# Other start addresses for the activation tiles of a chained attention, MoE and gated MoE kernel

## The chip, the core and the metric

The kernel runs on one core of one Trainium2 chip. The metric is the time of one execution on the device in microseconds, lower is better; two executions of the kernel before took 691.92 and 691.20 us, so its median is 691.56 us. Besides these there is one profiled execution, whose rows are read below.

## What is computed

Three layers follow each other. The attention has 2 batches, 8 heads, 768 positions and a head size of 64, with a window of 96 positions and 8 global ones; its output is a matrix of 1536 tokens by 512. Two feed-forward layers work on that matrix. Everything is in 32-bit floats.

```python
def _moe_ref(x, w_in, w_out):              # 512 -> 2048 -> 512
    h = x @ w_in
    g = h * (1.0 / (1.0 + np.exp(-h)))
    return (g @ w_out).astype(np.float32)

def _moe2_ref(x, w_gate, w_val, w_out):    # 512 -> 1536 -> 512
    gate = 1.0 / (1.0 + np.exp(-(x @ w_gate)))
    val = x @ w_val
    return (gate * val @ w_out).astype(np.float32)

x = attention(q, k, v).reshape(1536, 512)
out = _moe2_ref(_moe_ref(x, ...), ...)
```

## The kernel before

**Split numbers.** In the two feed-forward layers each 32-bit operand is kept as two `float32r` parts, a high part and a low part. A product is three matmuls: weight high by data high, weight high by data low, weight low by data high. `mm3` (line 501) issues such a triple. So the tiles of these layers have a middle axis of 2: `X[g]` is 128 x 2 x 4 x 512 (three of them, one for each group of 512 tokens), a weight tile `W[n]` is 128 x 2 x 512, a tile `g` of gated activations is 128 x 2 x 512.

**Stages.** In the first 70 us or so attention runs with a few matmuls of the first layer between. `warm_up` (line 893) puts matmuls of a zeroed bf16 tile, whose results nobody reads, between the pieces of attention in the first part. In the window that follows, attention and the first layer are interleaved by `PLAN`. After that `phase_rest` (line 630) runs the remaining tasks: A1 and A2 (first layer), B1 and B2 (second layer), each for groups of 512 tokens and chunks of 128 hidden columns. A task is an `H` and a `Y`. `H` multiplies `X[g]`, as the operand that is streamed (moving), by a weight tile that is held (stationary): 12 matmuls of 512 columns into one PSUM bank in A, 24 into two banks in B. `act1` or `act2` makes the tile `g` from it on ScalarE and VectorE. `Y` multiplies `g` by the output weights: 12 matmuls, three for each of four PSUM banks. In A the weight tile is held and `g` is streamed (line 680); in B `g` is held and the weight tile is streamed (line 682). The `Y` of a task is issued one or two tasks after its `H`. Every one of these matmuls has its own weight load.

**Which group runs when.** A1 runs with group 2 alone, from about 202 us; then the groups come in order: A2 with groups 0, 1, 2 (their `H` from 245, 289 and 333 us), B1 with 0, 1, 2 (from 377, 430 and 480 us), B2 with 0, 1, 2 (from 530, 580 and 630 us).

**Where the tiles lie.** Pools hand out SBUF in the order of allocation. Per partition, `X[g]` takes 16384 bytes, `acc` 8192, `nm_all` 12 x 8 x 4 = 384, a weight tile 4096, a stage tile 4096, a `u` or `sg` tile 2048, a `g` tile 4096. All but `nm_all` are multiples of 256 bytes, and `nm_all` lies between `X` and `W`. So every `X` tile lies 128 bytes from every weight tile, counted modulo 256, and every `g` tile lies at 0 from it. Slices inside a tile begin at multiples of 512 bytes, so this holds for every operand of every matmul. The weight tiles 16 to 23, allocated later, keep the same place modulo 256.

**What orders the work.** The code gives each engine's instructions in the order of the calls, and a scheduler that simulates engine times settles the order within the attention part.

The lines that the change touches are the allocation of `X` (line 75), `act1` (line 518) and `act2` (line 532), which allocate `g`:

```python
X = [main.tile([128, 2, KD, G], F32R, name=f"x{g}") for g in range(NG)]
gt = g_p.tile([128, 2, 512], F32R, tag="g", name="g")
```

Of the kernel before, what the change touches and what calls it, by code (L numbers as in the profile page):

```python
# [8 lines left out]
F32 = mybir.dt.float32  # L9
F32R = mybir.dt.float32r  # L10
# [22 lines left out]
def attn_moe_moe2_kernel(  # L33
# [14 lines left out]
    nc = tc.nc  # L48
# [5 lines left out]
    G = 512  # L54
    NG = NT // G
    BPG = G // 128
    KD = DM // 128
# [6 lines left out]
    main = fast.enter_context(tc.tile_pool(name="main", bufs=1))  # L64
    stage_p = fast.enter_context(tc.tile_pool(name="stage", bufs=3))
    u_p = fast.enter_context(tc.tile_pool(name="up", bufs=2))
    g_p = fast.enter_context(tc.tile_pool(name="gp", bufs=4))
# [4 lines left out]
    ident = const.tile([128, 128], F32, name="ident")  # L72
    nval = const.tile([128, 4], F32, name="nval")
    flag = const.tile([1, 1], I32, name="flag")
    X = [main.tile([128, 2, KD, G], F32R, name=f"x{g}") for g in range(NG)]
    acc = [main.tile([128, 4, 512], F32, name=f"acc{g}") for g in range(2)]
    nm_all = main.tile([128, NBLK, H], F32, name="nm_all")
    W = [main.tile([128, 2, 512], F32R, name=f"w{n}") for n in range(16)]
# [16 lines left out]
    def defer(n, fn):  # L95
        seq[0] += 1
        deferred.append((clock[0] + n, seq[0], fn))
# [359 lines left out]
    def take(n):  # L457
# [7 lines left out]
        pv = ps.rearrange("p (a b) -> p a b", a=NP)  # L465
        nc.scalar.activation(out=X[g][:, 0, :, xs], in_=pv, func=AF.Copy)
        nc.vector.tensor_tensor(X[g][:, 1, :, xs], pv, X[g][:, 0, :, xs].bitcast(F32), ALU.subtract)
        if 0 < i < BLK - 1:
# [28 lines left out]


    g_t = {}

    def mm3(ps, wl, wsl, xl, xsl, first, last, order=((0, 0), (0, 1), (1, 0))):
        for j, (a, b) in enumerate(order):
            nc.tensor.matmul(  # L503
                ps, wl[(slice(None), a) + wsl], xl[(slice(None), b) + xsl],
                start=(first and j == 0), stop=(last and j == len(order) - 1),
            )

    def h_units(g, key, ps, cols=slice(0, G), free=True):
        need_w(key)
        w = wtile(key)  # L510
        for kk in range(KD):
            def f(kk=kk):
                mm3(ps, w, (slice(kk * 128, (kk + 1) * 128),), X[g], (kk, cols), kk == 0, kk == KD - 1)
                if kk == KD - 1 and free and g == NG - 1:
                    done_w(key)
            yield f

    def act1(tag, ps, lo_pool):
        gt = g_p.tile([128, 2, 512], F32R, tag="g", name="g")
        g_t[tag] = gt  # L520
        sg = e_p.tile([128, 512], F32, tag="sg", name="sg")
        if lo_pool:
            nc.scalar.activation(out=sg, in_=ps, func=AF.Tanh, scale=0.5)
            nc.vector.scalar_tensor_tensor(out=sg, in0=sg, scalar=1.0, in1=ps, op0=ALU.add, op1=ALU.mult)
        else:
            nc.scalar.activation(out=sg, in_=ps, func=AF.Sigmoid)  # L526
            nc.vector.scalar_tensor_tensor(out=sg, in0=sg, scalar=2.0, in1=ps, op0=ALU.mult, op1=ALU.mult)  # L527
        nc.scalar.activation(out=gt[:, 0, :], in_=sg, func=AF.Copy)  # L528
        eng = nc.gpsimd if lo_pool else nc.vector
        eng.tensor_tensor(gt[:, 1, :], sg, gt[:, 0, :].bitcast(F32), ALU.subtract)  # L530

    def act2(tag, pg, pv):
        gt = g_p.tile([128, 2, 512], F32R, tag="g", name="g")
        g_t[tag] = gt
        sg = e_p.tile([128, 512], F32, tag="sg", name="sg")
        gf = sg
        nc.scalar.activation(out=sg, in_=pg, func=AF.Sigmoid)  # L537

        def rest():
            nc.vector.tensor_tensor(gf, sg, pv, ALU.mult)  # L540
            nc.scalar.activation(out=gt[:, 0, :], in_=gf, func=AF.Copy)  # L541
            nc.vector.tensor_tensor(gt[:, 1, :], gf, gt[:, 0, :].bitcast(F32), ALU.subtract)

        defer(4, rest)

    def macro(g, c0, n, col0):
# [13 lines left out]
        def sigs():  # L560
            if two:
                act1((tag, 0), bk["H"][c0 // 2 % 2], True)
            else:
                act1((tag, 0), bk["H"][0], True)
                act1((tag, 1), bk["H"][1], True)
# [64 lines left out]
    def phase_rest(prev):  # L630
# [9 lines left out]
        def H(ti):  # L640
            ph, g, c = tasks[ti]
            if ph[0] == "A":
                ps = bank[hi_[0] % 2]
                hi_[0] += 1
                for u in h_units(g, ("in", c), ps):
                    u()
                    unit()
                act1((ph, g, c), ps, False)
            else:
                pp = []  # L650
                for nm_ in ("gate", "val"):
                    ps = bank[hi_[0] % 4]
                    hi_[0] += 1
                    pp.append(ps)
                    for u in h_units(g, (nm_, c), ps):
                        u()
                        unit()
                act2((ph, g, c), pp[0], pp[1])
# [30 lines left out]
        def evac(ph, g, d, ps, ac):  # L689
# [3 lines left out]
            elif ph == "A2":  # L693
                nc.vector.tensor_tensor(a, a, ps, ALU.add)
                nc.scalar.activation(out=X[g][:, 0, d, :], in_=a, func=AF.Copy, scale=0.5)
                nc.vector.scalar_tensor_tensor(
                    out=X[g][:, 1, d, :], in0=a, scalar=0.5, in1=X[g][:, 0, d, :].bitcast(F32),
                    op0=ALU.mult, op1=ALU.subtract,
# [21 lines left out]
    def make_flag(ps):  # L720
        am = const.tile([128, 1], F32, name="am")
        ok = const.tile([1, 4], F32, name="ok")
        nc.vector.tensor_reduce(
            out=am, in_=nm_all.rearrange("p a b -> p (a b)"), op=ALU.max, axis=AX.X, apply_absolute_value=True
        )
# [234 lines left out]
```

## Time and profile before

| | |
|---|---|
| two timed executions | 691.92 and 691.20 us, median 691.56 us |
| span of the profiled execution, first to last instruction | 690.8 us |
| TensorE matmul busy | 676.4 us, 98% of the span |
| TensorE weight load busy | 539.7 us, 78% |
| VectorE busy | 374.2 us, 54% |
| ScalarE busy | 277.5 us, 40% |
| GpSimd busy | 84.6 us, 12% |

The profiled execution has no time of its own other than its span; the median of the timed ones lies 0.76 us above it. Engines are named PE (matmul), PEld (weight load), DVE (VectorE), ACT (ScalarE), POOL (GpSimd) and SP. A matmul's duration in a row runs from its start to its modelled end, and the next one starts before that end. What a matmul costs in a dense stream is therefore read from start to start, or from the chain of the work that ended last, where a piece of n matmuls is given without overlap.

### The profile page before, as it was taken

The numbers are of one execution on the slowest core, as the hardware profiler recorded it, in microseconds if no ns is written. First come the engines' busy times: TensorE is split into PE (matmuls) and PEld (weight loads), VectorE is DVE, ScalarE is ACT, GpSimd is POOL, SyncE is SP. The second block draws the span as 40 slices with busy tenths as digits, with TensorE's granted clock in tenths as the row PEclk, the third lists the DMA queues.
The fourth block names the chain that finished last, engine by engine and source line by source line (L and its number), as shares of the span: only waits on it lengthen the run. The fifth ranks groups of instructions, "written<-read, shape, count | busy, mean of one in ns | idle before, by whom it ended". The sixth has DMA issues, their size and how long they took to land.

```text
span 690.8 us, 9290 instructions
## 1 busy us (share of the span) xinstructions
PE 676.4 (98%) x3463; PEld 539.7 (78%) x3463; DVE 374.2 (54%) x869; ACT 277.5 (40%) x594; POOL 84.6 (12%) x166
## 2 busy tenths in 40 slices
PE   9999999999999999999999999999999999999995
PEld 7567886777778888888888888888888888888884
DVE  4999976534659999452499831211882311212112
ACT  3887865554645555332456521111451111111110
POOL 4255563342410000000000000000000000000000
PEclk9999999999999999999999999999999999999998
DMA  9766652210005554300025420000240000100101
GB/s 212 172 168 170 169 139 62 64 29 3 17 6 155 158 172 136 108 1 0 31 82 169 136 71 1 0 1 0 85 130 0 1 0 1 61 1 23 39 1 65
DMA packets 65301, 49.05 MB, mean 71 GB/s; under 512 B 39648, under 2 KB 60128, under 8 KB 65248
## 3 DMA queue, kind: packets, MB, share of 16 engines
q1 hardware_dynamic: 64032, 48.11, 24.7%
q8 instruction: 29, 0.48, 0.3%
q10 hardware_dynamic: 1216, 0.26, 0.2%
q14 instruction: 24, 0.20, 0.1%
HBM read 45.22 MB, written 3.15 MB: 70 GB/s over the span
## 4 chain that ended last, share of the span: by engine, by line
PE 94%; DVE 4%; issue 1%; ACT 0%; DVEq 0%
PE bank L503 54%; PE bank L682 14%; PE bank L680 13%; PE bank L377 4%; PE bank L449 3%; PE bank L428 2%; PE bank L895 2%; PE bank L340 1%; DVE t L392 1%; DVE acc L589 1%; DVE u L156 0%; DVE w L168 0%; DVE acc L701 0%; DVE ssum L405 0%; DVE u L159 0%
## 5 line engine op out<-in xcount | busy, mean ns | idle before, releaser
L503 PE MATMUL bank<-x,w 128*128 128x512 f32 (+1 forms) x1488 | 354.9, 389 | 0.0
L503 PEld LDWEIGHTS bank<-x,w 128*128 128x128 f32 x1488 | 272.6, 188 | 61.3 <-issue 0.8
L540 DVE TENSOR_TENSOR sg<-sg,bank 128x512 f32<-128x512 f32 x36 | 24.8, 688 | 167.7 <-PE bank L503 167.7
L682 PE MATMUL bank<-w,g 128*128 128x512 f32 x432 | 104.5, 390 | 0.0
L682 PEld LDWEIGHTS bank<-w,g 128*128 128x128 f32 x432 | 81.1, 188 | 17.8
L680 PE MATMUL bank<-g,w 128*128 128x512 f32 x384 | 93.0, 390 | 0.0
L680 PEld LDWEIGHTS bank<-g,w 128*128 128x128 f32 x384 | 72.1, 188 | 16.0
L537 ACT ACTIVATE sg<-bank 128x512 f32<-128x512 f32 x36 | 21.5, 597 | 120.5 <-PE bank L503 120.4
L541 ACT ACTIVATE g<-sg 128x512 fp32r<-128x512 f32 x36 | 22.8, 633 | 93.5 <-DVE sg L540 93.5
L503 PE MATMUL bank<-g,w 128*128 128x512 f32 (+1 forms) x240 | 54.0, 360 | 2.6 <-DVE acc L589 1.3
L154 ACT ACTIVATE u<-stage 128x512 f32<-128x512 f32 x68 | 45.7, 675 | 26.6 <-DVE w L168 26.1
L411 POOL TENSOR_SCALAR t<-t,ssum 128x256 f32<-128x256 f32 (+1 forms) x88 | 48.8, 569 | 61.4 <-DVE ssum L406 23.0
L168 DVE TENSOR_TENSOR w<-u,w 128x512 fp32r<-128x512 f32 x68 | 47.0, 693 | 12.0 <-ACT w L167 11.9
L167 ACT ACTIVATE w<-u 128x512 fp32r<-128x512 f32 x68 | 42.5, 629 | 26.6 <-PE bank L503 10.8
L399 ACT ACTIVATE t<-t,nm_all 128x256 f32<-128x256 f32 (+1 forms) x96 | 46.1, 484 | 17.0 <-DVE nm_all L392 17.0
L159 DVE SCALAR_TENSOR_TENSOR u<-stage,u 128x512 int32<-128x512 int32 x68 | 48.2, 709 | 0.3
L156 DVE SCALAR_TENSOR_TENSOR u<-stage,u 128x512 int32<-128x512 int32 x68 | 46.9, 689 | 0.6
L503 PEld LDWEIGHTS bank<-g,w 128*128 128x128 f32 x240 | 38.0, 189 | 10.6 <-DVE acc L589 3.8
L392 DVE CUSTOM_DVE_ANT_0 t<-bank,mask 128x256 f32<-128x256 f32 (+1 forms) x96 | 33.7, 396 | 17.6 <-PE bank L377 16.7
L528 ACT ACTIVATE g<-sg 128x512 fp32r<-128x512 f32 x48 | 30.3, 631 | 22.4 <-DVE sg L527 11.9
L527 DVE SCALAR_TENSOR_TENSOR sg<-sg,bank 128x512 f32<-128x512 f32 x32 | 21.9, 684 | 30.0 <-ACT sg L526 29.9
L526 ACT ACTIVATE sg<-bank 128x512 f32<-128x512 f32 x32 | 19.1, 596 | 42.9 <-PE bank L503 42.6
(90 smaller groups left out, 515.3 us busy)
## 6 DMA issues: line engine op xcount, KB each, us to landing
stage<-in_moe_w_out_dram SPq DMA_DIRECT2D x28, 512.0 KB, 3.6
stage<-in_moe_w_in_dram SPq DMA_DIRECT2D x16, 512.0 KB, 3.7
stage<-in_moe_w_gate_dram SPq DMA_DIRECT2D x12, 512.0 KB, 3.6
stage<-in_moe_w_val_dram SPq DMA_DIRECT2D x12, 512.0 KB, 3.5
v<-in_v_dram SPq DMA_DIRECT2D x12, 256.0 KB, 3.6
out_dram<-acc SPq DMA_DIRECT2D x12, 256.0 KB, 2.0
qk<-in_k_dram SPq DMA_DIRECT2D x11, 256.0 KB, 3.6
qk<-in_q_dram SPq DMA_DIRECT2D x11, 256.0 KB, 3.9
```

Source lines behind the costliest of these rows:

```text
L154: nc.scalar.activation(out=st, in_=hw.bitcast(F32), func=AF.Copy, scale=2.0 ** -112)
L156: nc.vector.scalar_tensor_tensor(out=ui, in0=lw, scalar=29, in1=ui, op0=ALU.logical_shift_right, op1=ALU.bitwise_or)
L159: nc.vector.scalar_tensor_tensor(out=ui, in0=hw, scalar=-2 ** 31, in1=ui, op0=ALU.bitwise_and, op1=ALU.bitwise_or)
L167: nc.scalar.activation(out=w[:, 0, :], in_=st, func=AF.Copy)
L168: nc.vector.tensor_tensor(w[:, 1, :], st, w[:, 0, :].bitcast(F32), ALU.subtract)
L392: nc.vector.tensor_tensor_reduce(t[:, e, 0:w], sp[e], mask[e][:, m0:m0 + w], op0=ALU.add, op1=ALU.min, scale=-c, scalar=3.0e38, accum_out= ...
L399: nc.scalar.activation(out=t[:, e, 0:w], in_=t[:, e, 0:w], func=AF.Exp, scale=-1.0, bias=nm_all[:, gi, 2 * p + e:2 * p + e + 1], accum_out ...
L411: nc.gpsimd.tensor_scalar(t[:, e, 0:w], t[:, e, 0:w], ss[:, e:e + 1], 1.0, op0=ALU.mult, op1=ALU.mult)
L503: nc.tensor.matmul(ps, wl[(slice(None), a) + wsl], xl[(slice(None), b) + xsl], start=(first and j == 0), stop=(last and j == len(order) - 1),)
L528: nc.scalar.activation(out=gt[:, 0, :], in_=sg, func=AF.Copy)
L680: nc.tensor.matmul(yb[d], w[:, a, sl], gt[:, b, :], start=st, stop=en)
L682: nc.tensor.matmul(yb[d], gt[:, a, sl], w[:, b, :], start=st, stop=en)
```

## The change

The three `X` tiles get a few unused floats in front (4, 52 and 24), a small tile `xend` that nothing reads stands behind them and is set to zero, and each `g` tile gets 64 floats more, of which the first 2, 40, 12 or 1 are left unused in turn. The views that the matmuls use begin behind the unused floats.

```diff
-    X = [main.tile([128, 2, KD, G], F32R, name=f"x{g}") for g in range(NG)]
+    X = []
+    for g, shift in enumerate((4, 52, 24)):
+        xb = main.tile([128, shift + 2 * KD * G], F32R, name=f"x{g}")
+        X.append(xb[:, shift:].rearrange("p (b k c) -> p b k c", b=2, k=KD))
+    xend = main.tile([128, 8], F32, name="xend")
+    nc.vector.memset(xend, 0.0)
@@
     g_t = {}
+    g_n = [0]
+
+    def g_tile():
+        shift = (2, 40, 12, 1)[g_n[0] % 4]
+        g_n[0] += 1
+        gb = g_p.tile([128, 1024 + 64], F32R, tag="g", name="g")
+        return gb[:, shift:shift + 1024].rearrange("p (b c) -> p b c", b=2)
@@ act1 and act2
-        gt = g_p.tile([128, 2, 512], F32R, tag="g", name="g")
+        gt = g_tile()
```

Counted modulo 256 from the weight tiles, the data then lies at:

| data | bytes before | bytes after |
|---|---|---|
| X[0] | 128 | 16 |
| X[1] | 128 | 240 |
| X[2] | 128 | 96 |
| g, every fourth tile from the 1st | 0 | 8 |
| g, from the 2nd | 0 | 160 |
| g, from the 3rd | 0 | 48 |
| g, from the 4th | 0 | 4 |

The program has one instruction more, the setting of `xend`. On ACT, POOL and SP the order of the instructions is the same, and on PE and DVE it is the same from the window with `PLAN` on. Ahead of that the scheduler's order differs in some places; line numbers are 5 or 12 higher in the changed file.

At the start of DVE, where the tile for `warm_up` is zeroed, stood before:

```order
L955 UNCONDITIONAL_BRANCH
L898 MEMSET warm 128x128
L251 CAST t<-t 128x384
L230 CAST nf<-nraw 128x4
L231 TENSOR_SCALAR nneg<-nf 128x2
```

and now:

```order
L967 UNCONDITIONAL_BRANCH
L80 MEMSET xend 128x8
L910 MEMSET warm 128x128
L256 CAST t<-t 128x384
L235 CAST nf<-nraw 128x4
L236 TENSOR_SCALAR nneg<-nf 128x2
```

The new memset stands ahead of the one for which PE's first matmul waits.

On PE, in the first part of attention, between scores (`kt`), transposes of queries and keys (`qk`) and filling matmuls (`warm`), stood before:

```order
L377 MATMUL bank_76<-kt_126 128x128
L377 MATMUL bank_77<-kt_126 128x128
L340 MATMUL bank_80<-ident,qk 128x128 x2
L895 LDWEIGHTS warm
L895 MATMUL bank_81<-warm 128x256
L377 MATMUL bank_76<-kt_127 128x128
L377 MATMUL bank_77<-kt_127 128x128
L340 MATMUL bank_82<-ident,qk 128x128 x2
```

and now:

```order
L382 MATMUL bank_76<-kt_128 128x128
L382 MATMUL bank_77<-kt_128 128x128
L345 MATMUL bank_80<-ident,qk 128x128 x2
L382 MATMUL bank_76<-kt_129 128x128
L382 MATMUL bank_77<-kt_129 128x128
L345 MATMUL bank_82<-ident,qk 128x128 x2
```

One filling matmul went from here to a later place, and at a few others a transpose of `qk` stands one or a few places earlier or later.

On DVE, where the softmax sums (`ssum`) are inverted between the steps that unpack weights (`u`), stood before:

```order
L155 TENSOR_SCALAR u<-u 128x512
L405 TENSOR_SCALAR ssum_136<-ssum_136 128x2
L156 SCALAR_TENSOR_TENSOR u<-stage,u 128x512
L406 RECIPROCAL ssum_136<-ssum_136 128x2
L405 TENSOR_SCALAR ssum_137<-ssum_137 128x2
L159 SCALAR_TENSOR_TENSOR u<-stage,u 128x512
```

and now:

```order
L160 TENSOR_SCALAR u<-u 128x512
L161 SCALAR_TENSOR_TENSOR u<-stage,u 128x512
L410 TENSOR_SCALAR ssum_138<-ssum_138 128x2
L410 TENSOR_SCALAR ssum_139<-ssum_139 128x2
L164 SCALAR_TENSOR_TENSOR u<-stage,u 128x512
L411 RECIPROCAL ssum_138<-ssum_138 128x2
```

The first sum is taken up one unpacking step later here.

## Rows read from the trace of the kernel before

**Rows 1.** The page: busy time, share of the span, instructions of each engine.

```profile
PE 676.4 (98%) x3463; PEld 539.7 (78%) x3463; DVE 374.2 (54%) x869; ACT 277.5 (40%) x594; POOL 84.6 (12%) x166
```

**Rows 2.** The page: chain that ended last, by engine and by line.

```profile
PE 94%; DVE 4%; issue 1%; ACT 0%; DVEq 0%
PE bank L503 54%; PE bank L682 14%; PE bank L680 13%; PE bank L377 4%; PE bank L449 3%; PE bank L428 2%; PE bank L895 2%; PE bank L340 1%; DVE t L392 1%; DVE acc L589 1%; DVE u L156 0%; DVE w L168 0%; DVE acc L701 0%; DVE ssum L405 0%; DVE u L159 0%
```

**Rows 3.** Groups of PE by shape: out<-streamed,held; count | busy us, mean ns | idle.

```profile
L503 PE MATMUL bank<-x,w 128*128 128x512 f32 x1392 | 340.1, 395 | 0.0
L682 PE MATMUL bank<-w,g 128*128 128x512 f32 x432 | 104.5, 390 | 0.0
L680 PE MATMUL bank<-g,w 128*128 128x512 f32 x384 | 93.0, 390 | 0.0
L503 PE MATMUL bank<-g,w 128*128 128x512 f32 x144 | 39.4, 406 | 1.7 <-DVE acc L589 1.3
...
L503 PE MATMUL bank<-x,w 128*128 128x256 f32 x96 | 14.8, 295 | 0.0
L503 PE MATMUL bank<-g,w 128*128 128x256 f32 x96 | 14.7, 292 | 0.9 <-DVE acc L587 0.9
```

**Rows 4.** Waits of PE: total us, times, longest; first and last of seven.

```profile
PE bank L503 <- DVE acc L589: 1.3, 4, 0.3
...
PE bank L340 <- DVE kt L351: 0.4, 1, 0.4
```

**Rows 5.** Stretches: length, busy us of PE, PEld, DVE, ACT, POOL, granted clock, DMA.

```profile
200.00:446.00 246.00, 246.00 (x1073) 200.14 (x1070) 162.20 (x278) 106.15 (x174) 0.00 (x0) 1.00 0.28 86
446.00:691.00 245.00, 236.77 (x1024) 191.84 (x1023) 75.08 (x119) 48.15 (x78) 0.00 (x0) 0.99 0.09 29
```

**Rows 6.** Chain in order of time, 225 to 262 us (A): start, us, what.

```profile
228.27 2.79 PE bank L503 x12
231.06 2.73 PE bank L680 x12
233.80 2.79 PE bank L503 x12
```

**Rows 7.** Chain in order of time, 500 to 530 us (B).

```profile
505.20 5.59 PE bank L503 x24
510.79 2.73 PE bank L682 x12
513.52 5.59 PE bank L503 x24
```

**Rows 8.** Timeline of PE, single starts around 513.5 us: start, us, what.

```profile
513.36 0.40 PE L503 MATMUL bank<-x,w 128*128 128x512 f32 x1
...
513.60 0.62 PE L503 MATMUL bank<-x,w 128*128 128x512 f32 x2
...
513.82 0.63 PE L503 MATMUL bank<-x,w 128*128 128x512 f32 x2
```

**Rows 9.** Chain in order of time, 0 to 14 us.

```profile
0.82 0.18 DVE warm L898
...
1.04 5.92 PE bank L895 x28
...
7.07 0.11 PE bank L895
...
8.05 1.86 PE bank L895 x17
```

**Rows 10.** Groups of PEld by shape: weight loads, count | busy us, mean ns.

```profile
L503 PEld LDWEIGHTS bank<-x,w 128*128 128x128 f32 x1488 | 272.6, 188 | 61.3 <-issue 0.8
...
L895 PEld LDWEIGHTS <-warm 128*128 128x128 bf16 x101 | 11.1, 112 | 4.2 <-DVE warm L898 1.0 <-issue 0.8
```

**Rows 11.** Longest waits from 200 us to the end: total us, times, longest.

```profile
DVE sg L540 <- PE bank L503: 167.7, 33, 6.3
ACT sg L537 <- PE bank L503: 120.4, 34, 4.2
```

**Rows 12.** Timeline of DVE, 17 to 20 us.

```profile
17.53 0.69 DVE L156 SCALAR_TENSOR_TENSOR u<-stage,u 128x512 int32<-128x512 int32 x1
```

More of the change, by code (lines that the diff above doesn't have):

```diff
@@ L532, in act2 @@
     def act2(tag, pg, pv):
-        gt = g_p.tile([128, 2, 512], F32R, tag="g", name="g")
+        gt = g_tile()
         g_t[tag] = gt
```

## The prediction

> **What bounds the kernel now.** I read the page's busy line first: PE is busy for 676.4 of 690.8 us, and no other engine for more than 54% [rows 1]. The chain that ended last says the same of the path: 94% of it is PE, and the lines of the two feed-forward layers (503, 680, 682) alone are 81% [rows 2]. Then I looked for waits of PE: there are seven kinds, the longest in total 1.3 us and the shortest 0.4 [rows 4]. Between 200 and 446 us PE is busy for all of 246.00 us, and from 446 us to the end for 236.77 of 245.00, at a granted clock of 1.00 and 0.99, so at the 2.4 GHz level throughout [rows 5]. So the time is the number of matmuls times what one costs in a dense stream. Only two things could move it much: fewer matmuls, which the change doesn't bring, or another cost of one.
>
> That cost is read from the chain in order of time. In A, 12 matmuls that stream `X` take 2.79 us and the 12 that stream `g` take 2.73 [rows 6], which is 232.5 and 227.5 ns for one. In B, 24 that stream `X` take 5.59 us, 233 ns for one, and 12 that stream the weights past a held `g` again 2.73, or 227.5 [rows 7]. All have 512 columns, one weight load of 128 columns, and the same clock; the mean durations, 395 against 390 ns, differ by the same 5 ns [rows 3]. So a matmul between `X` and `W` costs 5 ns more than one between `g` and `W`, whichever of the two is held. Where the tiles lie is one thing that divides the two kinds: 128 bytes apart modulo 256 in the first, 0 in the second. But it isn't the only one. `H` writes 12 matmuls running into one PSUM bank, `Y` three, and `X` and `g` are other tiles in another part of SBUF. The trace of before holds these two distances for dense streams and no third.
>
> Is there something to gain? A matmul of the zeroed bf16 tile with 256 columns costs 1.86 us for 17, 109.4 ns [rows 9]; 256 columns at 2.4 GHz are 106.7, so 2.7 ns are extra. A matmul of 512 would then be 213.3 + 2.7 = 216 ns. The streams of the two layers run 11.5 and 17 ns above that. Each weight load is shown with 188 ns in the `X` stream, where the bf16 one has 112 [rows 10], and lies under the matmul before it. So it is plausible, not shown, that reading 4-byte weights costs the running stream some cycles, more or fewer by where both lie.
>
> The Trainium skill, on the page "TensorE: Matmul & The Clock Gate", section "Part 2: What happens when you issue a matmul", says that PE has two independent read ports and that loading the next weights takes no bandwidth from the running matmul, with 215.7 ns for 512 columns. By that rule no start address could matter, and the time would stay as it is. The trace doesn't agree in the size: 227.5 and 233 ns.
>
> **The change, part by part.**
>
> *X tiles.* `H` has 1392 matmuls of 512 columns [rows 3]; by the code 432 of them stream X[0] (144 in A, 288 in B), 480 X[1] and 480 X[2] (192 and 288 each). X[0] comes to lie at 16 and X[1] at 240, which is 16 on the other side of 0; X[2] at 96, which is 32 from the old 128. I price each by the nearer of the two distances that rows show: X[0] and X[1] like `g` before, X[2] as before. In A that is (144 + 192) x (232.5 - 227.5) = 1.7 us, in B 576 x (233 - 227.5) = 3.2 us, together 4.9 us less.
>
> *g tiles.* 432 + 384 + 144 = 960 matmuls of 512 columns stream or hold a `g` [rows 3]. The tiles at 8 and 4 stay near 0, that at 48 is nearer to 0 than to 128, and that at 160 is 32 from 128: a quarter, 240, goes from 227.5 to 233, 1.3 us more.
>
> *Bounds of both.* Below, all extra is gone: 1392 x 17 + 960 x 11.5 = 34.7 us less. Above, I take the longest step that the `X` stream shows: its starts are 513.36, 513.60 and 513.82 [rows 8], steps of 0.24 and 0.22 us, so long and short ones lie within one stream. At 240 ns everywhere it is 1392 x 7 + 960 x 12.5 = 21.7 us more. The 192 matmuls of 256 columns are left at nothing: their mean durations, 295 and 292 ns [rows 3], differ by 3 ns, so by 0.3 us for 96.
>
> The Trainium skill's page "SBUF — State Buffer", section "Door 1: The DMA port swizzle", says that SBUF lines have 16 bytes and that each crossing to a new line is paid for. A `g` tile at 8 or 4 bytes begins inside a line, so a row of 2048 bytes touches 129 lines in place of 128; at 1/128 of 227.5 ns for half of 960 matmuls that is an estimate of 0.9 us more. No row of before shows such a tile.
>
> *Writers and readers of the moved tiles on ACT and DVE.* Their instructions are the same. If odd addresses made them longer, the cover is the wait for PE: from 200 us on DVE waits 167.7 us for `H` at line 540 alone and ACT 120.4 at 537 [rows 11]. A tile `g` is needed only after the next `H`, in B 5.59 us later. Priced at nothing.
>
> *The memset of `xend`* stands ahead of the one for which PE's first matmul waits, and that one takes 0.18 us [rows 9]. PE then runs 28 filling matmuls for 5.92 us before the first transpose, which needs loaded data; the memset delays filling, not data. Nothing, and 0.18 us without that cover.
>
> *Moved rows in attention.* A transpose or a filling matmul changes places with its neighbour, 0.11 us each [rows 9], and a softmax sum is taken up behind one unpacking step of 0.69 us more [rows 12]. Filling matmuls pad time that waits anyway. I take 0, with 0.7 us either way for the range.
>
> *Sum.* 690.8 - 4.9 + 1.3 = 687.2 us of span. The median of the timed runs lies 0.76 above the span, so 688.0 us.
>
> **The rivals.**
>
> *It doesn't do anything.* The 5 ns belong to the way `H` and `Y` use PSUM, or to the tiles' places at large, not to the distance modulo 256. For it: there are just two kinds, and they differ in all of these. Against it: `Y` in A and in B hold and stream opposite tiles and still agree to the row's 0.01 us. Time 691.6.
>
> *Only an exact 0 is cheap.* Then `X` gains nothing by a move from 128, and all of `g` loses its 0: 960 x 5.5 = 5.3 us more, 696.8. For it: `g` had the cheapest distance seen, and each of its new places leaves it. Against it: a move of one float can hardly matter as much as one of 128 bytes.
>
> *Any distance near 0 or off the multiples of 128 is cheap.* `X` gains on all three tiles (1.7 + 0.96 + 3.2 + 1.6 = 7.5 us by the same prices) and `g` loses nothing: 684.1.
>
> *Slower by over 2%.* Some of the places make streamed data and weights meet all through a load, and every matmul takes at least the long step. It decides from 13.8 us, 5.9 ns on each of 2352 matmuls; at 240 ns everywhere it is 713.3. For it: long steps exist. Against it: they alternate with short ones, and it would have to hold for most of seven places.
>
> *Faster by over 2%.* The extra goes altogether: 691.6 - 34.7 = 656.9. Against it: neither stream of before comes anywhere near 216 ns.
>
> **How the numbers follow.** Forecast by the nearer distance 0.38, with a range of its own of 686 to 690 (the 0.7 us of attention, 0.9 for either stream). No effect 0.27. Only 0 is cheap 0.17. All of `X` gains 0.08. Slower by over 2% 0.05, faster by over 2% 0.05. The predicted time is that of the first, 688.0 us. From 684 to 697 us the first four cases lie, 0.90 together; the unknown costs of a few tiles spread over the same stretch, so I make it no narrower. Two per cent, about what a measurement of this kernel can tell from no change, is 13.8 us: faster 0.05, same 0.90, slower 0.05.
>
> **What would show it.** In the chain in order of time of the changed kernel, each stage has its own distance: the pieces of 24 that stream `X` in B1 and B2 should be 5.46 us with groups 0 and 1 and stay 5.59 with group 2. Pieces of 12 in `Y` should be 2.73 us three times out of four and 2.79 the fourth time. If all pieces keep 5.59 and 2.73, the distance is not what divides the streams. If groups 0 and 1 keep 5.59 while `Y` grows everywhere, only an exact 0 is cheap. A piece of 24 above 5.76 us (240 ns) or below 5.2 (216 ns) would be outside of what I bound. New waits of PE above a few tenths would mean that ACT or DVE lost their cover, which I priced at nothing.

## The result

The changed kernel takes 695.69 us, median of two runs (695.18 and 696.20), against 691.56 before: 1.0063 times as long, 95% interval 1.0044 to 1.0082. It became slower by 0.6%, where 688.0 us, 0.5% faster, had been forecast. This ratio and those below are the ones on record; dividing the medians gives slightly other values, here 1.0060. The span of the profiled execution is 694.4 us after 690.8, so 3.6 us longer.

The page of the changed kernel, busy time and the chain that ended last, to be held against [rows 1, 2]:

```profile
PE 680.7 (98%) x3463; PEld 541.0 (78%) x3463; DVE 373.5 (54%) x870; ACT 277.7 (40%) x594; POOL 83.1 (12%) x166
...
PE 94%; DVE 4%; issue 0%; ACT 0%; DVEq 0%
```

Nothing changed in what bounds the kernel. PE is busy 4.3 us longer with the same 3463 matmuls; the other engines stay within 1.5 us of where they were. Its waits (who waited for whom, total us, times, longest) are those of [rows 4], and none is new:

```profile
PE bank L515 <- DVE acc L601: 1.3, 4, 0.3
PE bank L907 <- DVE warm L910: 1.1, 1, 1.1
```

So it is the single matmul that costs more. The groups of PE by shape (count, busy us, mean ns), to be held against [rows 3]:

```profile
L515 PE MATMUL bank<-x,w 128*128 128x512 f32 x1392 | 340.8, 396 | 0.0
L694 PE MATMUL bank<-w,g 128*128 128x512 f32 x432 | 106.4, 395 | 0.0
L692 PE MATMUL bank<-g,w 128*128 128x512 f32 x384 | 95.2, 396 | 0.0
```

Before, the two `Y` groups had 390 ns and `H` 395; now all three have 395 or 396. The chain in order of time says where. First A (225 to 262 us), to be held against [rows 6]; line 515 is `H`, 692 is `Y`:

```profile
227.85 2.80 PE bank L515 x12
230.65 2.85 PE bank L692 x12
233.50 2.80 PE bank L515 x12
236.30 2.79 PE bank L692 x12
```

Then B, with X[2] at 96 bytes (500 to 530 us), to be held against [rows 7]; line 694 is `Y`:

```profile
505.00 2.79 PE bank L694 x12
507.79 5.60 PE bank L515 x24
513.39 2.80 PE bank L694 x12
```

and B with X[0] at 16 bytes (556 to 577 us):

```profile
557.99 5.57 PE bank L515 x24
563.55 2.77 PE bank L694 x12
```

and with X[1] at 240 bytes (595 to 625 us):

```profile
599.92 5.67 PE bank L515 x24
605.59 2.80 PE bank L694 x12
```

Over all of the trace the pieces of `Y` went from 2.73 us to between 2.76 and 2.86, whichever of the four places their `g` tile has. The pieces of `H` stayed near 5.59: 5.57, 5.67 and 5.60 us for the three groups. Taken over all steps from start to start from the first matmul of A1 on (201.8 us before, 201.2 now), `Y` costs 4.2 us more (1.9 where weights are streamed, 2.3 where `g` is) and `H` 0.55 (X[0] 0.5 less, X[1] 0.9 more, X[2] 0.15 more); the attention before it takes 0.6 us less and the end after the last matmul 0.5 less. These add up to the 3.6 us. The last two are scatter: over all kernels of this document, the stretch ahead of A1 takes 201.0 to 202.2 us and the end 7.1 to 8.9.

### The profile page after: what moved, and what is told of

Same layout as the page of the kernel before. It is cut to its first block, busy times and chain, and to the rows that moved or that the text cites. A ratio compares the mean times of both kernels' runs of the same rounds, so it can differ in the third digit from the quotient of the medians.

```text
span 694.4 us, 9291 instructions
## 1 busy us (share of the span) xinstructions
PE 680.7 (98%) x3463; PEld 541.0 (78%) x3463; DVE 373.5 (54%) x870; ACT 277.7 (40%) x594; POOL 83.1 (12%) x166
## 4 chain that ended last, share of the span: by engine, by line
PE 94%; DVE 4%; issue 0%; ACT 0%; DVEq 0%
PE bank L515 54%; PE bank L694 14%; PE bank L692 13%; PE bank L382 4%; PE bank L454 3%; PE bank L433 2%; PE bank L907 2%; PE bank L345 1%; DVE t L397 1%; DVE acc L601 1%; DVE u L161 0%; DVE w L173 0%; DVE u L164 0%; DVE acc L713 0%; DVE ssum L410 0%
## 5 line engine op out<-in xcount | busy, mean ns | idle before, releaser
L694 PE MATMUL bank<-w,g 128*128 128x512 f32 x432 | 106.4, 395 | 0.0
L692 PE MATMUL bank<-g,w 128*128 128x512 f32 x384 | 95.2, 396 | 0.0
```

The lines of the kernel that those rows point to most:

```text
L692: nc.tensor.matmul(yb[d], w[:, a, sl], gt[:, b, :], start=st, stop=en)
L694: nc.tensor.matmul(yb[d], gt[:, a, sl], w[:, b, :], start=st, stop=en)
```

## The experiments

Theory D: the place of the tiles modulo 256 decides what a matmul costs, and equal places are the one cheap case. Its rivals: the nearer-distance rule of the prediction; S, by which the streams of `H` and `Y` differ for other reasons; A, by which the streamed operand's own place decides. Unless it says otherwise, 32 floats behind `nm_all` move the weight tiles and `g` by 128 bytes, which brings them level with where `X` lay before.

### All at the same place

```diff
-    nm_all = main.tile([128, NBLK, H], F32, name="nm_all")
+    nm_room = main.tile([128, NBLK * H + 32], F32, name="nm_all")
+    nm_all = nm_room[:, 0:NBLK * H].rearrange("p (a b) -> p a b", a=NBLK)
```

> The kernel before with 32 unused floats behind nm_all, so that X, g and the weight tiles all lie at the same place modulo 256; nothing else moves. Theory D (the distance decides; equal places are the one cheap case, 227.5 ns for a matmul of 512 columns, all others 231 to 237): the 1392 matmuls that stream X fall from 233 to 227.5 ns, pieces of 24 in B from 5.59 to 5.46 us, and the time to about 684 us. Theory S (the 5 ns between the streams of H and Y belong to the way they use PSUM, or to the tiles themselves): pieces stay 5.59 and 2.73 us, 691.6 us. Theory A (the place of the streamed operand alone decides, and 128 modulo 256, where g and W lay before, is the cheap one): now everything begins at 0, Y rises to about 2.80 us a piece and H stays, about 697 us.

682.76 us, 0.9864 times the kernel before (0.9845 to 0.9883). Groups of PE, then the chain in A and in B:

```profile
L504 PE MATMUL bank<-x,w 128*128 128x512 f32 x1392 | 332.3, 390 | 0.0
L683 PE MATMUL bank<-w,g 128*128 128x512 f32 x432 | 103.9, 389 | 0.0
```

```profile
227.15 2.72 PE bank L504 x12
229.87 2.72 PE bank L681 x12
...
507.31 5.44 PE bank L504 x24
512.75 2.72 PE bank L683 x12
```

`H` and `Y` now cost the same to 0.01 us, 226.7 ns a matmul. S has fallen: nothing but the 128 bytes in the place of the weights and of what lies behind them set the two apart. A has fallen for the place 128, since all begin at 0 here. This kernel, with one line more than the one before, is faster than the kernel before and the changed one.

`Y` fell too, from 228.0 to 226.7 ns a matmul on average in B, though its own distance was 0 before. The reason is in the starts of the kernel before: the first three steps of a `Y` behind an `H` take 232, 232 and 231 ns, and only the other nine 226 or 227. So a step depends on those that ran ahead of it, and the 227.5 ns of `Y` before were a mixture.

### All moved together

```diff
+    for g, (shift, room) in enumerate(((24, 64), (24, 64), (24, 64))):
+        xb = main.tile([128, room + 2 * KD * G], F32R, name=f"x{g}")
+        X.append(xb[:, shift:shift + 2 * KD * G].rearrange("p (b k c) -> p b k c", b=2, k=KD))
...
+    nm_room = main.tile([128, NBLK * H + 56], F32, name="nm_all")
```

> As all0, but X, g and the weight tiles all lie 96 bytes further, so that their distance is still 0 modulo 256 and their own place is another (X[0] and X[2] come to 256 modulo 512 from the weights, X[1] to 0). Theory D with a period of 256: as all0, about 684 us, all pieces of 24 at 5.46 us. D with a period of 512: group 1 cheap, groups 0 and 2 at 5.59 us or above, about 689. Theory A (the streamed operand's own place): all streams at 5.59 and 2.80 us or so, about 697 us. Theory S: 691.6 us.

681.63 us, 0.9850 times (0.9832 to 0.9868). Its chain with X[0] and with X[1]:

```profile
556.66 5.44 PE bank L507 x24
...
597.46 5.44 PE bank L507 x24
```

It is the distance, not the own place, and X[0], 256 bytes off modulo 512, is as cheap as X[1] at 0. So 256 bytes apart is as good as 0. No run shows whether other distances repeat after 256 bytes too.

### The change in two halves

The change's `g_tile` alone, all else as before, without the 32 floats:

```diff
+    def g_tile():
+        shift = (2, 40, 12, 1)[g_n[0] % 4]
...
-        gt = g_p.tile([128, 2, 512], F32R, tag="g", name="g")
+        gt = g_tile()
```

> The change's g tiles alone: 8, 160, 48 and 4 bytes from the weight tiles, X stays at 128 as before. Theory D: nearly the whole loss of the change is here; 960 matmuls rise by 4 to 5 ns, pieces of Y go from 2.73 to about 2.79 us, and the time to 695 to 696.5 us. The nearer-distance rule of the prediction: only the tiles at 160 rise, 692.9 us. Theory S: 691.6 us.

696.14 us, 1.0057 times (1.0036 to 1.0077). Its chain in B with X[0]:

```profile
556.14 2.78 PE bank L690 x12
558.92 5.60 PE bank L511 x24
564.52 2.77 PE bank L690 x12
```

The change's three `X` places alone, `g` level with the weights:

```diff
+    for g, (shift, room) in enumerate(((4, 64), (60, 64), (24, 64))):
+        xb = main.tile([128, room + 2 * KD * G], F32R, name=f"x{g}")
+        X.append(xb[:, shift:shift + 2 * KD * G].rearrange("p (b k c) -> p b k c", b=2, k=KD))
```

> The change's X tiles alone: 16, 240 and 96 bytes from the weight tiles, g stays at 0 as before. Theory D: X[0] gains about 1 ns a matmul, X[1] loses about 2, X[2] stays, so the time stays within 1 us, 690.6 to 692.6 us. The nearer-distance rule: X[0] and X[1] fall to 227.5 ns, 686.7 us. Theory S: 691.6 us with all pieces of 24 at 5.59 us.

692.31 us, 1.0009 times (0.9999 to 1.0018). Its chain in B with groups 0, 1 and 2:

```profile
563.88 5.56 PE bank L507 x24
...
597.14 5.60 PE bank L507 x24
...
647.16 5.61 PE bank L507 x24
```

The loss of the change is in its `g` tiles: they alone give 1.0057 of its 1.0063, the `X` tiles alone an interval that reaches from 0.9999 to 1.0018. The `X` tiles left one dear place for three others. At 240 bytes a piece takes 5.60 us here and 5.67 in the changed kernel. Two things differ between them: the `Y` that runs between, and the distance modulo 512, which by the order of allocation is 240 here and 496 there. X[0] lies at 272 modulo 512 in both and takes 5.56 and 5.57 us, whatever its `Y`, which speaks for the second; no run separates the two.

### Other distances

```diff
-    X = [main.tile([128, 2, KD, G], F32R, name=f"x{g}") for g in range(NG)]
+    X = []
+    for g, (shift, room) in enumerate(((8, 64), (16, 64), (48, 64))):
+        xb = main.tile([128, room + 2 * KD * G], F32R, name=f"x{g}")
+        X.append(xb[:, shift:shift + 2 * KD * G].rearrange("p (b k c) -> p b k c", b=2, k=KD))
```

This is the first of four such kernels, with 32, 64 and 192 bytes. The others differ in the shifts alone.

> All weight and g tiles as in all0, X at 32, 64 and 192 bytes from the weight tiles (groups 0, 1, 2). Theory P (a short period: what repeats every 64 or 32 bytes is as good as 0): groups 1 and 2 run pieces of 24 in 5.44 us, group 0 too if it is 32; time about 684 (64) or 682 us (32). Theory Z (only 0 modulo 256 is cheap): all pieces of 24 at 5.54 to 5.68 us, time 689 to 692 us.

691.85 us, 1.0003 times (0.9993 to 1.0013). Its chain in B with groups 0, 1 and 2:

```profile
555.50 5.60 PE bank L507 x24
...
597.14 5.51 PE bank L507 x24
...
646.94 5.60 PE bank L507 x24
```

```diff
-    for g, (shift, room) in enumerate(((8, 64), (16, 64), (48, 64))):
+    for g, (shift, room) in enumerate(((1, 64), (2, 64), (3, 64))):
```

> All weight and g tiles as in all0, X at 4, 8 and 12 bytes from the weight tiles, so within one 16-byte line of the equal place. If a place within the same 16 bytes is as good as 0: pieces of 24 at 5.44 us for all groups and about 682 us. If only the exact 0 is cheap: pieces of 24 at 5.54 us or above already from one float on, 688 to 692 us.

692.88 us, 1.0020 times (1.0009 to 1.0031). The same three rows at 4, 8 and 12 bytes:

```profile
556.43 5.71 PE bank L507 x24
...
598.46 5.60 PE bank L507 x24
...
640.03 5.50 PE bank L507 x24
```

```diff
-    for g, (shift, room) in enumerate(((8, 64), (16, 64), (48, 64))):
+    for g, (shift, room) in enumerate(((15, 64), (18, 64), (19, 64))):
```

> All other tiles as in all0, X at 60, 72 and 76 bytes from the weight tiles. If some other place is as cheap as 0 or cheaper, the neighbourhood of 64 and a rest of 12 in 16 are the places where the runs so far point (5.54 to 5.60 us at 64 by single steps, 5.50 at 12): a piece of 24 at 5.44 us or below in one of the groups. If 0 alone is cheap: 5.50 to 5.71 us in all three.

688.99 us in one run, against 691.05 in one run of the kernel before. At 60, 72 and 76 bytes:

```profile
561.45 5.48 PE bank L507 x24
...
603.06 5.65 PE bank L507 x24
...
644.79 5.51 PE bank L507 x24
```

```diff
-    for g, (shift, room) in enumerate(((8, 64), (16, 64), (48, 64))):
+    for g, (shift, room) in enumerate(((63, 64), (61, 64), (28, 64))):
```

> All other tiles as in all0, X at 252, 244 and 112 bytes from the weight tiles, so 4 and 12 on the other side of 0. If only how far the two lie apart counts, not which is ahead, 252 takes 5.71 us for a piece of 24 like 4, and 244 takes 5.50 like 12. If the sign counts: 252 below 5.65 or 244 above 5.55 us. 112 as 96 and 128, 5.59 us.

691.72 us in one run. At 252, 244 and 112 bytes:

```profile
563.38 5.52 PE bank L507 x24
...
596.75 5.71 PE bank L507 x24
...
647.10 5.54 PE bank L507 x24
```

A piece of 24, divided by 24, over all distances that ran:

| bytes modulo 256 | ns | bytes | ns | bytes | ns |
|---|---|---|---|---|---|
| 0 | 226.7 | 32 | 233.3 | 112 | 230.8 |
| 4 | 237.9 | 60 | 228.3 | 128 | 232.9 |
| 8 | 233.3 | 64 | 229.6 | 192 | 233.3 |
| 12 | 229.2 | 72 | 235.4 | 240 | 233.3 to 236 |
| 16 | 232 | 76 | 229.6 | 244 | 237.9 |
| | | 96 | 233.3 | 252 | 230.0 |

Of 17 distances 0 is the cheapest. Next to it, at one float, lies one of the two dearest, 4 and 244. There is no slope towards 0 to follow, and the sign counts: 4 and 252 are as far from 0, and 7.9 ns apart. (Modulo 512 they lie at 260 and 508, by the order of allocation.) Theory P fell, since no piece came to 5.44 us. "0 alone is cheap" holds in that no other distance is as cheap, but its ranges were missed: 64, 12 and 60 bytes took 5.51, 5.50 and 5.48 us, all below what it asked for, and the kernel at 4, 8 and 12 bytes took 0.9 us more than the 692 it allowed. 112 took 5.54 where 5.59 was expected.

What sorts the distances better, read off afterwards and not tested on new ones, is the remainder modulo 16. A remainder of 4 (4 and 244) gives 237.9 ns, 8 (8 and 72) 233.3 and 235.4, and 12 (12, 60, 76 and 252) 228.3 to 230.0. The multiples of 16 spread from 226.7 to 236, in no order that these runs show. The streamed `g` tiles agree: in A of the changed kernel every fourth one, at 4 bytes, is the one whose piece of 12 takes 2.85 us or a little more, so 237.5 ns or more a matmul.

### Shorter weight loads

```diff
+            wj = slice(wsl[0].start, wsl[0].start + 64) if j in half else wsl[0]
             nc.tensor.matmul(
-                ps, wl[(slice(None), a) + wsl], xl[(slice(None), b) + xsl],
+                ps[0:64, :] if j in half else ps, wl[:, a, wj], xl[(slice(None), b) + xsl],
...
-                mm3(ps, w, (slice(kk * 128, (kk + 1) * 128),), X[g], (kk, cols), kk == 0, kk == KD - 1)
+                mm3(ps, w, (slice(kk * 128, (kk + 1) * 128),), X[g], (kk, cols), kk == 0, kk == KD - 1, half=(1, 2) if kk < KD - 1 else (1,))
```

First on the kernel before, without the 32 floats, so with X at 128 bytes:

> The kernel before (X at 128, g at 0), but in H the second of three matmuls, and the third but for the last of a bank, hold 64 weight columns in place of 128; the other 64 columns of these two products are left out, so that part of the computation is missing. Their weight loads are half as long. That is 7 of 12 loads in H. Theory L (reading the next weights takes cycles from the running stream): the extra of 17 ns over 216 halves at 7 of 12 steps, so a piece of 24 takes 14 x 8.5 = 0.12 us less, 5.47 us, and the kernel about 685 us. Theory F (the extra is a fixed cost of a matmul with 4-byte data, or of changing weights): 5.59 us and 691.6 us.

690.74 us in one run. Its chain in B:

```profile
596.03 5.53 PE bank L504 x24
601.56 2.77 PE bank L683 x12
```

Then with all level:

> The same halving of 7 of 12 weight loads in H, on all0 (X and g at 0); the same part of the computation is left out. Theory L: the extra of 11 ns over 216 halves at 7 of 12 steps, a piece of 24 takes 14 x 5.5 = 0.08 us less than 5.44, 5.36 us, and the kernel about 678 us. Theory F: 5.44 us and 682 us.

686.27 us in one run. Its chain in B:

```profile
600.68 5.51 PE bank L505 x24
606.18 2.73 PE bank L684 x12
```

With 7 of 12 loads halved, `H` costs 230.4 ns at 128 bytes, 2.5 less than before, and 229.6 with all level, 2.9 more than with whole loads. Both theories fail: L asked for 5.47 and 5.36 us, F for 5.59 and 5.44. So with shorter loads a stream became dearer, and the extra isn't a sum of cycles in proportion to the loads. The edit halves the columns that a matmul works on as well as those that are loaded, and the runs don't separate the two. At 128 bytes the untouched `Y` rose too, from 2.73 to 2.77 us.

### The two parts of a tile at two places

```diff
+    def g_tile():
+        gb = g_p.tile([128, 1088], F32R, tag="g", name="g")
+        return gb.rearrange("p (b c) -> p b c", b=2)[:, :, 0:512]
```

> As all0, but the low part of each g tile lies 128 bytes further, so at 128 from everything else. In B, Y holds g high, g high, g low in turn and streams weights that all lie at 0. Theory N (what counts is the distance of the streamed data to the weights that are loaded for the next matmul meanwhile): the step behind the second of each three is the dear one, about 233 ns, and the one behind the third stays at 227. Theory H (the distance to the weights that are held): the step behind the third is the dear one. In both the pieces of 12 in Y grow from 2.72 to about 2.75 us and the time from 682 to about 685 us; pieces of 24 stay 5.44.

685.63 us in one run. Its chain in B:

```profile
509.33 5.44 PE bank L509 x24
514.77 2.77 PE bank L688 x12
```

`Y` grew by 0.05 us, where both theories had 0.03, and the pieces of 24 on line 509, as in the kernel with all level, stayed. Worked out from the starts in the trace, the steps of the `Y` that begins at 514.61 us, in ns, with what is held and what is being loaded meanwhile:

```
held high, high is loaded   227   227   226   227
held high, low is loaded    232   233   233   232
held low, high is loaded    234   234   234   234
```

Theory H by itself would have left the second row at 227, but all of it rose; so the distance to the weights that are being loaded counts. But the third rose too, with the next load back at 0. Either the held ones count as well, or a dear step passes some of its cost on to the next; the run can't tell these two apart. That cost can be passed on is shown elsewhere: three steps of `Y` at 231 or 232 ns behind `X` at 128 in the kernel before. Behind X[1] at 240, with the change's `X` places alone, there is none: 227, 227, 226 from the first step on.

## Why the prediction was wrong

**What bounds the kernel**: right. The time is the number of matmuls times the cost of one, at the same clock (0.994 to 0.999 in all runs). Against the kernel before, that cost moved the spans by 8.9 us less to 4.7 us more, and all the rest together by 1.9 us at most.

**Does the distance decide?** Right, and shown only now: all level brought `H` down to `Y` (5.59 to 5.44 us), so the 5 ns between them were the distance, and "it doesn't do anything" fell. The 227.5 ns that I took as the price of distance 0 was three dear steps and nine at 226.7, so 0 is cheaper and 128 further from it than I read. The Trainium skill, on the page "TensorE: Matmul & The Clock Gate", section "Part 2: What happens when you issue a matmul", has the next weights loaded without a cost to the running matmul. These runs don't agree: the same instructions in the same order cost 226.7 to 237.9 ns by the start address alone, and with the two parts of `g` at two places a step rose from 227 to 232 or 233 ns when nothing but the weights loaded meanwhile lay at another place.

**The X term, 4.9 us less**: this is the step that failed. I priced each new place by the nearer of two known distances, and there is no such nearness. X[0] at 16 gave 5.57 us in place of 5.46, X[1] at 240 gave 5.67, dearer than at 128. Only X[2] came as priced, 5.60 for 5.59. In place of 4.9 us less the three groups cost 0.55 us more.

**The g term, 1.3 us more**: failed by the same step. Not one tile in four rose but all; the pieces read 2.76 to 2.86 us where three in four should have kept 2.73. 4.2 us more in place of 1.3. The estimate that the Trainium skill's page "SBUF — State Buffer", section "Door 1: The DMA port swizzle", allowed for a start inside a 16-byte line was 0.9 us. The runs show no such small surcharge: in `H` 4 bytes cost 11 ns a matmul and 12 bytes 2.5, while 16, on a line's start, costs 5.

**The rival that came nearest** is "only an exact 0 is cheap", with 0.17 and 696.8 us. It has the right step, the loss in every `g` tile, but not to the letter: it takes one price for all other distances, and they cost 228.3 to 237.9 ns. What I held against it, that one float can hardly matter as much as 128 bytes, was a belief about smoothness with no row behind it. In fact one float matters more, 237.9 ns against 232.9. I should have seen that two points, of which one was the cheapest cost in the trace, carry no interpolation, and that the change leaves that point with every `g` tile.

**The covers**: right. The chain in order of time at the start of the changed kernel, to be held against [rows 9]:

```profile
0.80 0.07 DVE xend L80
0.86 0.17 DVE warm L910
...
1.07 5.78 PE bank L907 x27
```

The memset of `xend` took 0.07 us, and the filling matmuls behind it are 27 in place of 28, so it delayed filling alone. No new wait of PE appeared, so ACT and DVE kept theirs. The moved rows of attention cost nothing that shows, the stretch ahead of A1 being 0.6 us shorter, within the 0.7 I allowed and within the scatter of the runs. The bounds of 216 and 240 ns for a stream held in all of the runs, the upper one by luck: I read the step from starts rounded to 10 ns, and it takes 234, while single steps reach 241 in that kernel's B and 247 in others. From span to median I added 0.76 us; the two runs of the changed kernel have 1.8 us between span and time each, so the pairing of one execution's span with other executions' median was off by about 1 us, which decides nothing here.

## What to carry to other kernels

Where dense streams of 4-byte matmuls bound a kernel, compare start to start between streams of equal shape; a few ns there were worth more here than any wait of PE, the longest kind of which came to 1.3 us in total. Then look at where streamed and held tiles lie modulo 256, and try all of them level: here 128 bytes of padding brought 1.4%, and none of the 16 other distances was as good. Don't price an untried address by its neighbours; a small odd-sized tile allocated between two large ones, as `nm_all` is here, decides it unseen.

## What the runs showed of the hardware

Single steps of one stream, worked out from the starts (resolution 1 ns), at four distances. They are from the kernels with all level (0), with `X` at 32, 64 and 192 (64), before (128) and with the change's `X` places alone (240):

```
  0 bytes   226 226 228 226 226 227 227 226 227 226
 64 bytes   229 232 226 229 232 226 229 231 226 229
128 bytes   237 229 238 229 238 229 237 229 238 229
240 bytes   233 234 233 233 234 233 233 234 233 233
```

These four streams settle into cycles of one, two or three steps. The sum over a cycle is a multiple of 6.667 ns within the resolution: 226.67 is 34 of them, 233.33 is 35, 237.5 + 229.2 is 70, 229 + 232 + 226 is 103. Not all streams are so plain: at 32 bytes the cycle has four steps (231, 235, 234, 234), and at 4, 8 and 60 bytes no cycle as short as these can be read in a piece of 24. So the start of a matmul seems to be held to a beat, and the distance, with what ran before, seems to decide which cycle follows. That would fit with half a load costing more than a whole one, and with `Y` taking three dear steps behind `X` at 128 and none at 240; it is an inference from the sums at a few distances, not tested by itself. What the beat is, and what is waited for at it, no run here shows.
